# K of the last eight attention units turned on VectorE, and the phase-2 weight conversions begun one chunk earlier

## The chip, the cores and the metric

The kernel runs on one core of a Trainium2 chip. Five engines with queues of their own work side by side: TensorE (PE; its weight loads are shown apart as PEld), VectorE (DVE), ScalarE (ACT), GpSimd (POOL) and SyncE (SP), which here does nothing but issue DMAs. Within a queue instructions run in order. The metric is device time: 1471.89 us, the median of three runs (1470.66 to 1473.28).

## The reference

Three blocks follow each other, all in float32: a two-step attention through 32 packed vectors per head, a mixer with a token shift, and a mixer over tokens and channels. The first block is the one that changes:

```
def sm_attn(qq, kk, vv):
    s = scale * matmul(qq, kk.T)          # then softmax over the last axis
    return softmax(s) @ vv
p_packed = sm_attn(p, k, v)               # p: 8 x 8 x 32 x 64; k, v: 8 x 8 x 576 x 64
out = sm_attn(q, p_packed, p_packed)      # q: 8 x 8 x 576 x 64
x = out.transpose(0, 2, 1, 3)             # heads side by side: 8 x 576 x 512
k2 = relu(xk @ w_k); v2 = k2*k2 @ w_v; r = sigmoid(xr @ w_r); y = r * v2
u = y + token mixing of y with U, V;  result = u + relu(u @ w_ch1) @ w_ch2
```

`xk` and `xr` are mixes of `x` with `x` one token earlier.

## The kernel before

**Attention** is cut into 16 units, numbered by (pair of batches `bp`, pair of heads `j`): a unit has two batches times two heads. For one unit K (576 x 64 per head) has to stand with its 64 dims on the partitions before it is multiplied with the packed queries P; this turned K is the tile `kh`. Every unit loads K with four DMAs (`load_k`, L612): two of 256 KB in runs of 1 KB, two of 32 KB for the last 64 tokens. TensorE turns it: eight 128x128 transposes into two PSUM banks (L682 to L688), which ScalarE or VectorE copy to `kh`, and two 64-column transposes for the tail, copied to a part of the tile `at` (called `kt`, L690 to L696). One more transpose turns P (`pbd` to `pT`). Then come the scores (`psat<-kh,pT`, `psat<-at,pT`), their maxima, the exponentials (`a1`), and so on to `xo`, which is stored to `x_d`.

For Q the two halves of the units differ. Units 0 to 7 ("plain", `u < NPLAIN`) turn Q on TensorE too. Units 8 to 15 load Q with eight DMAs of 72 KB in runs of 128 bytes, 32 dims of one head per 32 partitions (L633 to L641), so that VectorE's transpose of 32x32 blocks (`plan.turn`, two instructions a unit) gives the layout wanted.

**The mixer** runs over 12 chunks of 384 columns (three chunks per pair of batches). A chunk has the matmul groups `psr` (36 matmuls of 512 columns), `psk` (96 of 384) and `psv` (72 of 512), and `psu`. The first four units run ahead of the mixer. Units 4 to 7 are mixed in among the matmuls of chunk 0 on, units 8 to 11 from chunk 3 on, units 12 to 15 from chunk 6 on in the program, but on the queues they stand earlier, since the last eight have the highest class (`cls = 0`, L1408).

**Casts.** The weights of phase 2 (`V`, `w_ch1`, `w_ch2`, 34 pieces) come as float64 and are converted on the side: a DMA brings a piece to a tile `st` (three buffers), ScalarE takes its absolute value, VectorE makes float32 of the bits in some six integer and float instructions with tiles `a` and `m` (two buffers each), and a DMA stores `m` to `v_d` or `w_d` (`Cast.run`, L894). From chunk `CAST0` = 2 on each chunk has `NPER` = 5 of these in its lowest class (`cls = 3`).

**Phase 2** (from about 690 us) is a chain of matmuls `psc`, with `w_d` turned into seven sums per block (`ws_d`) during chunks 7 to 10.

**What sets the order.** All instructions are recorded first and then ordered by a list scheduler (`Plan.emit`, L346) that simulates the five queues: each engine takes the ready instruction of the lowest class; TensorE and SyncE take the earliest recorded within a class. Copies out of PSUM may go to ScalarE or VectorE, whichever is free. The order that results is fixed in the program. A tile's buffers come free when its last reader is done: a unit's K tile is loaded again for the next unit once its transposes have read it. DMAs of SyncE share eight semaphores in turn, so that a DMA is issued when the eighth before it has landed.

Of the kernel before, what the change touches and what calls it, by code (L numbers as in the profile page):

```python
# [9 lines left out]
F32 = mybir.dt.float32  # L10
# [3 lines left out]
AF = mybir.ActivationFunctionType  # L14
# [470 lines left out]
def packed_attention_moe_mixer_kernel(  # L485
# [18 lines left out]
    B, H, S, D = q.shape  # L504
    NP = p.shape[2]
    P = 128
# [15 lines left out]
    NPLAIN = 2 * NJ  # L522
    SCALE = 1.0 / float(D) ** 0.5
# [3 lines left out]
    plan = Plan(nc)  # L527
# [37 lines left out]
    def ps_att():  # L565
        return plan.bank(att_banks[0], "psat", att_banks[0] is ps_a)
# [17 lines left out]
    class Bufs:  # L584
# [22 lines left out]
            return self.kept[1:]  # L607

        def tile_in(self, tag):
            return plan.tile(self.big_p, [P, 1152], F32, "big", parts=tuple(range(8)), name=tag)  # L610

        def load_k(self, u, after=()):  # L612
            bp, j = divmod(u, NJ)
            if u not in self.kin:
                self.kin[u] = self.tile_in("kin")
            t = self.kin[u]
            for b2 in range(2):
                src = k[2 * bp + b2, 2 * j:2 * j + 2]
                plan.dma(
                    t.at(b2)[:, b2 * 512:(b2 + 1) * 512].rearrange("p (h t d) -> p h t d", t=4, h=2),  # L620
                    src[:, 0:512, :].rearrange("h (p t) d -> p h t d", t=4), after=after)
            for b2 in range(2):
                src = k[2 * bp + b2, 2 * j:2 * j + 2]
                plan.dma(
                    t.at(2 + b2)[b2:P:2, 1024:1152].rearrange("p (h d) -> p h d", h=2),
                    src[:, 512:576, :].rearrange("h s d -> s h d"), after=after)
# [37 lines left out]
    def attention_steps(A, u, u_next):  # L664
        bp, j = divmod(u, NJ)
        kin, qin, vin = A.kin.pop(u), A.qin.pop(u), A.vin.pop(u)
# [3 lines left out]
        plain = u < NPLAIN  # L670
        kh = A.big(F32, "kh")
        qt, at = A.big(F32, "qt"), A.big(F32, "at", (0, 1))
        pT, ppz = A.keep(plain)
# [5 lines left out]
        if early:  # L679
            claim()  # L680

        for b2 in range(2):  # L682
            yield
            ps = ps_att()
            for n in range(4):
                plan.transpose(ps[:, n * P:(n + 1) * P],
                               kin.at(b2)[:, b2 * 512 + n * P:b2 * 512 + (n + 1) * P], ident)
            plan.copy(kh[:, b2 * 512:(b2 + 1) * 512], ps)  # L688
        yield
        ps = ps_att()  # L690
        for h in range(2):
            plan.transpose(ps[0:64, h * P:(h + 1) * P], kin[:, 1024 + h * 64:1088 + h * 64], ident)
        plan.transpose(ps[:, 2 * P:3 * P], A.pbd.rearrange("p h d -> p (h d)"), ident)
        kt = at.at(1)[:, 640:896].rearrange("p (h c) -> p h c", h=2)
        plan.copy(kt[0:64].rearrange("p h (b c) -> p h b c", b=2),
                  ps[0:64, 0:2 * P].rearrange("p (h c b) -> p h b c", h=2, b=2))  # L696
        plan.copy(pT, ps[:, 2 * P:3 * P].rearrange("p (b c) -> p b c", b=2))
        if early:
            A.load_k(u_next, A.after)
# [1 line left out]
        st = A.st  # L701
        yield
        sps = [ps_att() for _ in range(2)]
        for b2 in range(2):
            for h in range(2):
                o = slice(b2 * 64 + h * 32, b2 * 64 + (h + 1) * 32)
                for r in range(2):
                    rows = slice(r * 64, (r + 1) * 64)
                    plan.mm(sps[r][o, 0:256], pT[rows, b2, h * 32:(h + 1) * 32],
                            kh[rows, b2 * 512 + h * 256:b2 * 512 + (h + 1) * 256],  # L710
                            start=True, stop=True, skip_group_check=True)
        for b2 in range(2):
            for h in range(2):
                o = slice(b2 * 64 + h * 32, b2 * 64 + (h + 1) * 32)
                plan.mm(sps[0][o, 256:320], pT[0:64, b2, h * 32:(h + 1) * 32],
                        kt[0:64, h, b2 * 64:(b2 + 1) * 64], start=True, stop=True, skip_group_check=True)
        s0, s1 = st.at(0), st.at(1)
        plan.reduce(s0[:, 0:1], sps[0][:, 0:320], ALU.max)
        plan.reduce(s0[:, 1:2], sps[1][:, 0:256], ALU.max)
# [1 line left out]
        a1 = A.a1  # L721
        bias = st.at(0)[:, 3:4]
        for r in range(2):
            plan.act(a1[:, 0:512].rearrange("p (n r c) -> p n r c", n=2, r=2)[:, :, r, :],
                     sps[r][:, 0:256].rearrange("p (n c) -> p n c", n=2), AF.Exp,
                     st.at(1)[:, 4 + r:5 + r], bias, SCALE)
        for b2 in range(2):
            r = slice(b2 * 64, (b2 + 1) * 64)
            plan.act(a1[r, 512 + b2:640:2], sps[0][r, 256:320], AF.Exp,
                     st.at(1)[r, 6:7], bias[r], SCALE)  # L730
        plan.reduce(s0[:, 8:9], s1[:, 4:8], add)
        plan.recip(s0[:, 9:10], s0[:, 8:9])

        for c in range(3 if plain else 0):
            yield
            ps = ps_att()
# [3 lines left out]
            n = 3 if c < 2 else 2  # L740
# [6 lines left out]
        if not plain:  # L747
            yield
            for b2 in range(2):
                r = slice(b2 * S, (b2 + 1) * S)  # L750
# [5 lines left out]
        ps = ps_att()  # L756
# [4 lines left out]
        ps = ps_att()  # L761
# [4 lines left out]
        ps = ps_att()  # L766
        for t in range(5):
            for g in range(4):
                o = t * P + g * 32
# [3 lines left out]
                        start=(t == 0), stop=(t == 4), skip_group_check=True)  # L773
# [3 lines left out]
        if not plain:  # L777
            for b2 in range(2):
                r = slice(b2 * 64, (b2 + 1) * 64)
# [5 lines left out]
        ps = ps_att()  # L785
# [13 lines left out]
        if plain:  # L799
# [25 lines left out]
            ps = ps_att()  # L825
# [4 lines left out]
            ps = ps_att()  # L830
            plan.transpose(ps[:, 0:P], a2f[:, 512:640], ident)
            for b2 in range(2):
                r = slice(b2 * 64, (b2 + 1) * 64)
                plan.copy(th[r, 512:576], ps[r, r])
        else:
            n = S // NP
            a2 = plan.tile(A.one, [P, 20, NP], F32, "a2", parts=(0, 1))[:, 0:n, :]
            s2 = plan.tile(A.one, [P, 4, 20], F32, "s2", parts=(0, 1))
            for g, (c0, c1) in enumerate(halves):
                yield  # L840
                ps = ps_att()
# [19 lines left out]
        for c0, c1 in halves:  # L861
            w = c1 - c0
            if plain:
                yield
                pss = [ps_att() for _ in range(2)]
                for b2 in range(2):
                    r = slice(b2 * 64, (b2 + 1) * 64)
# [13 lines left out]
    def attention(A, u, u_next):  # L881
        for _ in attention_steps(A, u, u_next):
            pass
# [83 lines left out]
    for what in FIRST.split():  # L967
        u = int(what[1])
# [14 lines left out]
    plan.cls = 0  # L983
    A0.after = go
    steps = [attention_steps(AX_[u], u, NJ if u == 0 else None) for u in range(NLEAD)]
    step = 0
    while any(s is not None for s in steps):
# [36 lines left out]
    for b2 in range(2):  # L1024
        r = slice(b2 * 64, (b2 + 1) * 64)
# [7 lines left out]
    for i0, i1 in ((0, NI),):  # L1033
        src = uv[:, i0 * NP:i1 * NP]
# [145 lines left out]
    def tmp_tile():  # L1180
        i = count["tmp"] % 6
        count["tmp"] += 1
        if i < 3:
            return plan.tile(m_p, [P, CW], F32, "m", name="tmp")[:, 0:256]
        return plan.tile(tr_p, [P, 256], F32, "tmp")
# [148 lines left out]
    def product(q, f, i, name, fresh):  # L1334

        if fresh:
            bank_abc[name] = plan.bank(ps_c1, "psc1")
        ps = bank_abc[name][:, 0:256]
        w, x = load_ws(f, i), ops[q][i]
        n = 0  # L1340
        for k in range(2):
            for wi, a in PASS:
                plan.mm(ps, half(w, wi)[:, k * P:(k + 1) * P],
                        half(x, a).rearrange("p (a k c) -> p k a c", a=4, k=2)[:, k],
                        start=(fresh and n == 0), stop=(n == 5), skip_group_check=True)
                n += 1
        return ps
# [34 lines left out]
            plan.dma(v_d[:, c * 288:(c + 1) * 288], w[0:NP, 0:288])  # L1382
        casts.append((slice(0, NP), V[:, c * 288:(c + 1) * 288], 288, put_v))
    NCAST, FIRST_WS = 9, 7
    CAST0, NPER = 2, 5
    for m in range(MC):
        def put1(w, m=m):
            plan.dma(w1_d[m], w)
# [16 lines left out]
    for n in range(len(chunks)):  # L1405
        b, c = chunks[n]
# [27 lines left out]
        if n >= CAST0:  # L1434
            plan.cls = 3
            for _ in range(len(casts) if n == NCAST else NPER):
                if casts:
                    rows, src, size, put = casts.pop(0)
# [27 lines left out]
    for q in range(NQ):  # L1466
# [12 lines left out]
        for f in range(NF):  # L1479
# [9 lines left out]
            b = product(q, f, 1, "b", True)  # L1489
            s = tmp_tile()  # L1490
            plan.tt(s, p1, b, add)
            c = product(q, f, 2, "c", True)
# [68 lines left out]
```

## Time and profile before

| | |
|---|---|
| three runs | 1470.66, 1471.89, 1473.28 us |
| profiled execution | 1469.44 us |
| span of its instructions | 1467.7 us |
| TensorE, weight loads | 1434.1 us busy (98%), 1259.5 us (86%) |
| VectorE, ScalarE, GpSimd | 988.5 us (67%), 716.2 us (49%), 268.8 us (18%) |
| DMA | 294.53 MB, 201 GB/s in the mean |

The profiled execution takes 1.7 us more than the span of its instructions. TensorE's busy time counts matmuls from their start to a modelled end, so that it says little about free time; the spacing of the weight loads, one per matmul, says more. By the stores of `xo` the units 8 to 15 follow each other from 218.4 us to 475.8 us, each about 32 us long.

### The profile page before, as it was taken

The numbers are of one execution on the slowest core, as the hardware profiler recorded it, in microseconds if no ns is written. First come the engines' busy times: TensorE is split into PE (matmuls) and PEld (weight loads), VectorE is DVE, ScalarE is ACT, GpSimd is POOL, SyncE is SP. The second block draws the span as 40 slices with busy tenths as digits, with TensorE's granted clock in tenths as the row PEclk, the third lists the DMA queues.
The fourth block names the chain that finished last, engine by engine and source line by source line (L and its number), as shares of the span: only waits on it lengthen the run. The fifth ranks groups of instructions, "written<-read, shape, count | busy, mean of one in ns | idle before, by whom it ended". The sixth has DMA issues, their size and how long they took to land.

```text
span 1467.7 us, 25586 instructions
## 1 busy us (share of the span) xinstructions
PE 1434.1 (98%) x9104; PEld 1259.5 (86%) x9104; DVE 988.5 (67%) x2147; ACT 716.2 (49%) x1519; POOL 268.8 (18%) x519
## 2 busy tenths in 40 slices
PE   6799999999999999999999999999999999999998
PEld 5678888888888988889899999899998999999997
DVE  6999577888788888885665465556546554554533
ACT  5777656776666677664443333333223332333322
POOL 0000000000000000100333333333333333333331
PEclk8889999999999999999999999999999999999999
DMA  8864355666552877841999988899998789879763
GB/s 232 254 193 123 97 137 137 188 175 179 158 158 94 291 246 248 255 153 59 308 261 249 225 231 215 212 258 225 230 230 212 204 220 247 208 215 237 202 179 79
DMA packets 235709, 294.53 MB, mean 201 GB/s; under 512 B 91200, under 2 KB 126336, under 8 KB 235584
## 3 DMA queue, kind: packets, MB, share of 16 engines
q1 hardware_dynamic: 163008, 160.76, 37.8%
q0 software_dynamic: 72576, 132.15, 35.6%
q8 instruction: 73, 1.20, 0.3%
q14 instruction: 52, 0.43, 0.1%
HBM read 231.94 MB, written 60.89 MB: 200 GB/s over the span
## 4 chain that ended last, share of the span: by engine, by line
PE 90%; DMA 3%; DVE 3%; SPq 2%; ACT 1%; issue 1%; DVEq 0%; ACTq 0%
PE psc L197 50%; PE psk L197 13%; PE psv L197 13%; PE psr L197 7%; PE psat L197 4%; PE psat L209 2%; SPq L319 2%; PE psu L197 1%; DMA kin<-in_k_dram 1%; PE psh L197 1%; DMA st<-in_moe_w_k_dram 1%; DMA ut<-uq_d 0%; DMA st<-in_moe_w_v_dram 0%; DMA uq_d<-ux 0%; DMA w_d<-m 0%
## 5 line engine op out<-in xcount | busy, mean ns | idle before, releaser
L197 PE MATMUL psc<-w,hid 128*128 128x512 f32 x1728 | 421.1, 391 | 0.4 <-DVE hid L273 0.4
L197 PEld LDWEIGHTS psc<-ob,wb 128*128 128x128 f32 x3024 | 387.4, 191 | 13.4
L197 PE MATMUL psc<-ob,wb 128*128 128x256 f32 x3024 | 392.0, 283 | 0.0
L319 POOL DMA_DIRECT2D wb<-ws_d x504 | 266.9, 530 | 647.6 <-PE psc L197 401.5
L197 PEld LDWEIGHTS psc<-w,hid 128*128 128x128 f32 x1728 | 314.6, 188 | 60.6 <-DVE hid L273 1.5
L233 ACT ACTIVATE hid<-tmp 128x256 fp32r<-128x256 f32 x216 | 131.5, 676 | 231.0 <-DVE tmp L254 231.0
L197 PE MATMUL psk<-xk,wk 128*128 128x384 f32 x1152 | 227.1, 340 | 0.4 <-ACT sq L233 0.4
L197 PE MATMUL psv<-wv,kk 128*128 128x512 f32 x864 | 226.3, 397 | 0.0
L197 PEld LDWEIGHTS psk<-xk,wk 128*128 128x128 f32 x1152 | 201.3, 188 | 11.1 <-issue 2.6
L197 PEld LDWEIGHTS psv<-wv,kk 128*128 128x128 f32 x864 | 158.6, 188 | 32.9 <-issue 3.0
L273 DVE SCALAR_TENSOR_TENSOR hid<-tmp,hid 128x256 fp32r<-128x256 f32 x216 | 127.2, 633 | 54.6 <-ACT hid L233 54.1
L273 DVE SCALAR_TENSOR_TENSOR hid<-psc,hid 128x256 fp32r<-128x256 f32 x72 | 45.3, 629 | 167.4 <-ACT hid L233 167.4
L254 DVE TENSOR_TENSOR tmp<-tmp,psc 128x256 f32<-128x256 f32 x288 | 112.9, 409 | 61.7 <-PE psc L197 61.7
L233 ACT ACTIVATE hid<-psc 128x256 fp32r<-128x256 f32 x72 | 45.8, 636 | 157.3 <-PE psc L197 157.3
L197 PE MATMUL psr<-wr,xr 128*128 128x512 f32 x432 | 114.5, 406 | 2.0 <-DVE xr L291 1.6
L197 PEld LDWEIGHTS psr<-wr,xr 128*128 128x128 f32 x432 | 81.9, 194 | 21.3 <-DVE xr L291 2.1
L288 ACT ACTIVATE tmp<-psc 128x256 f32<-128x256 f32 x144 | 57.2, 397 | 58.7 <-PE psc L197 50.7
L233 ACT ACTIVATE sq<-psk 128x384 f32<-128x384 f32 x96 | 46.8, 489 | 75.1 <-PE psk L197 74.7
L311 POOL MEMSET x<- 128x8 f32 x4 | 0.4, 112 | 429.7 <-DVE m L270 249.2
L254 DVE TENSOR_TENSOR kk<-sq,kk 128x384 fp32r<-128x384 f32 x96 | 52.6, 549 | 25.1 <-ACT kk L288 24.6
L233 ACT ACTIVATE m<-x,om_t 128x384 f32<-128x384 f32 x96 | 55.3, 607 | 4.9 <-DVE xr L254 3.8
L270 DVE SCALAR_TENSOR_TENSOR m<-x,mu_t,m 128x384 f32<-128x384 f32 x96 | 56.4, 608 | 0.3 <-ACT m L233 0.2
(157 smaller groups left out, 1500.6 us busy)
## 6 DMA issues: line engine op xcount, KB each, us to landing
wb<-ws_d POOLq DMA_DIRECT2D x504, 256.0 KB, 4.0
st<-in_moe_w_ch_dram SPq DMA_DIRECT2D x32, 512.0 KB, 5.3
ws_d<-wb SPq DMA_DIRECT2D x56, 256.0 KB, 4.0
x_d<-xo SPq DMA_DIRECT2D x16, 576.0 KB, 3.8
x_d<-x SPq DMA_DIRECT2D x36, 256.0 KB, 2.6
kin<-in_k_dram SPq DMA_DIRECT2D x32, 256.0 KB, 4.5
vin<-in_v_dram SPq DMA_DIRECT2D x32, 256.0 KB, 4.8
x<-x_d SPq DMA_DIRECT2D x8, 1024.0 KB, 5.8
```

Source lines behind the costliest of these rows:

```text
L197: self.nc.tensor.matmul(o, l, r, start=start, stop=stop, **k)
L209: self.nc.tensor.transpose(out.get(), in_.get(), ident.get())
L233: self.nc.scalar.activation(o, in_.get(), func, **k)
L254: return self.elem(engs, lambda e, o, x, y: e.tensor_tensor(out=o, in0=x, in1=y, op=op), out, [a, b], self.TT, cls)
L270: ("dve",), lambda e, o, x, y, z: e.scalar_tensor_tensor(out=o, in0=x, scalar=z, in1=y, op0=op0, op1=op1), out, [a, b, s], {"dve": (1.042, ...
L273: ("dve",), lambda e, o, x, y: e.scalar_tensor_tensor(out=o, in0=x, scalar=s, in1=y, op0=op0, op1=op1), out, [a, b], self.TT, cls)
L288: self.nc.scalar.activation(o, i, AF.Copy)
L311: (self.nc.gpsimd if eng == "pool" else self.nc.vector).memset(o, 0.0)
L319: (self.nc.sync if eng == "sp" else self.nc.gpsimd).dma_start(out=o, in_=i)
```

## The change

Units 8 to 15 load K as they load Q: in runs of 128 bytes, 32 dims of a head on 32 partitions. That takes 24 DMAs a unit, 16 of 32 KB and 8 of 8 KB, in place of four. One transpose of VectorE over the whole tile (128 x 1152) gives `kh`, tail included; the ten transposes on TensorE, two of the three PSUM banks of the stage and the three copies of K go. The columns of `kh` come out in another order than before, so the scores read other rows for the second batch, and the exponentials write their results with a stride that restores the order. P is still turned on TensorE. Apart from this, `CAST0` is 1: the casts begin in chunk 1, five a chunk as before.

```
         def tile_in(self, tag):
-            return plan.tile(self.big_p, [P, 1152], F32, "big", parts=tuple(range(8)), name=tag)
+            return plan.tile(self.big_p, [P, 1152], F32, "big", parts=tuple(range(24)), name=tag)
...
+            if u >= NPLAIN:
+                for b2 in range(2):
+                    for h in range(2):
+                        src = k[2 * bp + b2, 2 * j + h]
+                        main = src[0:512].rearrange("(p n r) (e s) -> r e p n s", p=32, r=2, e=2)
+                        c0 = (2 * b2 + h) * 256
+                        for g in range(4):
+                            plan.dma(t.at(8 * b2 + 4 * h + g)[g * 32:(g + 1) * 32, c0:c0 + 256]
+                                     .rearrange("p (n s) -> p n s", s=32), main[g // 2 ^ b2, g % 2], after=after)
+                        tail = src[512:S].rearrange("(p n) (e s) -> e p n s", n=2, e=2)
+                        c0 = 1024 + h * 64
+                        for e in range(2):
+                            g = 2 * b2 + e
+                            plan.dma(t.at(16 + 4 * b2 + 2 * h + e)[g * 32:(g + 1) * 32, c0:c0 + 64]
+                                     .rearrange("p (n s) -> p n s", s=32), tail[e], after=after)
+                return
...
-        for b2 in range(2):
+        for b2 in range(2 if plain else 0):
             yield
             ps = ps_att()
...
         yield
+        if not plain:
+            plan.turn(kh, kin)
         ps = ps_att()
-        for h in range(2):
+        for h in range(2 if plain else 0):
             plan.transpose(ps[0:64, h * P:(h + 1) * P], kin[:, 1024 + h * 64:1088 + h * 64], ident)
         plan.transpose(ps[:, 2 * P:3 * P], A.pbd.rearrange("p h d -> p (h d)"), ident)
...
+                    rows = slice(b2 * 64, (b2 + 1) * 64)
+                    tail = kh[rows, 1024 + h * 64:1088 + h * 64]
...
+                to = to.rearrange("p n (c m) -> p m n c", m=4)
+                s = s.rearrange("p (m n c) -> p m n c", m=4, n=2)
+            plan.act(to, s, AF.Exp, st.at(1)[:, 4 + r:5 + r], bias, SCALE)
...
-    CAST0, NPER = 2, 5
+    CAST0, NPER = 1, 5
```

How the order moves is shown at three places, all around unit 9, first the one before, then the one of the changed kernel.

TensorE's queue before, from the K transposes of unit 9 (`ident,kin`) to its scores (`kh,pT` and, for the tail, `at,pT`); `psv` and `psr` are the mixer's:

```order
L209 MATMUL psat<-ident,kin 128x128 x8
L197 MATMUL psv<-wv_1113,kk 128x512 x4
L197 MATMUL psr<-wr_200,xr 128x512
L209 MATMUL psat<-ident,kin 64x128 x2
L209 MATMUL psat<-ident,pbd 128x128
L197 MATMUL psr<-wr_200,xr 128x512 x2
L197 MATMUL psr<-wr_201,xr 128x512 x3
L197 MATMUL psr<-wr_202,xr 128x512
L197 MATMUL psat<-kh,pT 32x256 x8
L197 MATMUL psat<-at,pT 32x64 x4
```

The same place now, from the last matmuls of unit 8 (`th,wide`) to unit 9's scores:

```order
L197 MATMUL psat<-th,wide 128x256 x3
L197 MATMUL psr<-wr_202,xr 128x512 x2
L209 MATMUL psat<-ident,pbd 128x128
L197 MATMUL psv<-wv_1114,kk 128x512 x4
L197 MATMUL psr<-wr_202,xr 128x512
L197 MATMUL psat<-kh,pT 32x256 x8
L197 MATMUL psat<-kh,pT 32x64 x4
```

The ten transposes of K are gone and only that of `pbd` is left between the units; the tail's scores now read `kh`.

VectorE's queue before, where unit 9's second half of K is copied (`kh<-psat`, then the tail `at<-psat`), up to the maxima of its scores (`st<-psat`); `st<-a` and `a<-a` belong to a cast, `m` and `xr` to the mixer:

```order
L264 TENSOR_SCALAR st<-a 128x512
L264 TENSOR_SCALAR a<-a 128x512
L291 COPY kh<-psat 128x512
L270 SCALAR_TENSOR_TENSOR m<-x,mu_t,m 128x384 x2
L291 COPY at<-psat 64x256
L270 SCALAR_TENSOR_TENSOR m<-x,mu_t,m 128x384
L254 TENSOR_TENSOR xr<-m,xr 128x384
L277 TENSOR_REDUCE st<-psat 128x1
L254 TENSOR_TENSOR xr<-m,xr 128x384
L277 TENSOR_REDUCE st<-psat 128x1
```

VectorE's queue now, where unit 9's K is turned; `pp`, `wide`, `a_2845` and `s_2826` are unit 8's:

```order
L270 SCALAR_TENSOR_TENSOR pp<-psat,st,hmask 128x128
L254 TENSOR_TENSOR kk<-sq,kk 128x384
L254 TENSOR_TENSOR wide<-pp,wide 64x128 x2
L215 STREAM_TRANSPOSE kh<-kin 128x1152
L215 STREAM_TRANSPOSE a_2845<-psat 128x320
L215 STREAM_TRANSPOSE a_2845<-psat 128x256
L270 SCALAR_TENSOR_TENSOR m<-x,mu_t,m 128x384
L277 TENSOR_REDUCE s_2826<-a_2845 128x18
```

The one transpose of K has moved about half a unit ahead: it stands in the middle of unit 8, in front of unit 8's own turned scores.

SyncE's queue before, from the store of unit 7's `xo` on: K and Q of unit 9 (`kin`, `qin`), then x of a chunk, a cast's load (`st`) and store (`v_d`):

```order
L319 DMA x_d_66<-xo 128x1152
L319 DMA kin<-in_k_dram 128x2x256 x2
L319 DMA kin<-in_k_dram 64x2x64 x2
L319 DMA qin<-in_q_dram 32x18x32 x8
L319 DMA x<-x_d_66 128x384
L319 DMA x<-x_d_66 128x2x63
L319 DMA st<-in_moe_w_ch_dram 128x4x256
L319 DMA v_d<-m 32x288
L319 DMA st<-in_moe_w_ch_dram 128x4x256
L319 DMA vin<-in_v_dram 128x2x256
```

SyncE's queue now, at K and Q of unit 9:

```order
L319 DMA kin<-in_k_dram 32x8x32 x4
L319 DMA kin<-in_k_dram 32x2x32 x2
L319 DMA kin<-in_k_dram 32x8x32 x4
L319 DMA kin<-in_k_dram 32x2x32 x2
L319 DMA kin<-in_k_dram 32x8x32 x4
L319 DMA kin<-in_k_dram 32x2x32 x2
L319 DMA kin<-in_k_dram 32x8x32 x4
L319 DMA kin<-in_k_dram 32x2x32 x2
L319 DMA qin<-in_q_dram 32x18x32 x8
L319 DMA x_d_66<-xo 128x1152
L319 DMA st<-in_moe_w_ch_dram 128x4x256 x2
L319 DMA w_d_81<-m 128x512
```

K's four DMAs have become 24, and what follows them, the store of `xo`, two cast loads and a cast's store (`w_d_81`), stands behind 32 DMAs of K and Q where it stood behind 12.

## Rows read from the trace of the kernel before

**Rows 1.** the page's chain that ended last: shares of the span by engine.

```profile
PE 90%; DMA 3%; DVE 3%; SPq 2%; ACT 1%; issue 1%; DVEq 0%; ACTq 0%
```

**Rows 2.** busy time by stage: window, length, engines (instructions), clock, DMA share, GB/s.

```profile
135.10:195.30 60.20, 59.74 (x393) 48.90 (x392) 38.59 (x90) 36.27 (x83) 0.00 (x0) 1.00 0.38 105
218.40:475.80 257.40, 254.40 (x1788) 214.73 (x1787) 215.64 (x477) 172.19 (x383) 0.32 (x2) 1.00 0.54 156
250.80:283.90 33.10, 32.20 (x223) 26.43 (x222) 28.77 (x63) 24.74 (x53) 0.00 (x0) 1.00 0.66 192
564.40:607.30 42.90, 42.90 (x212) 38.20 (x211) 38.49 (x88) 29.81 (x64) 5.42 (x10) 1.00 0.91 284
```

**Rows 3.** weight loads by form, 218 to 476 us: busy, mean ns, idle before.

```profile
L197 PEld LDWEIGHTS psk<-xk,wk 128*128 128x128 f32 x448 | 77.9, 188 | 4.8 <-issue 1.1 <-ACT sq L233 0.7
...
L209 PEld LDWEIGHTS psat<-ident,kin 128*128 128x128 f32 x64 | 7.4, 140 | 1.2 <-ACT xo L288 0.4
L209 PEld LDWEIGHTS psat<-ident,kin 128*64 128x64 f32 x16 | 1.8, 110 | 0.9
...
L209 PEld LDWEIGHTS psat<-ident,pbd 128*128 128x128 f32 x8 | 1.1, 140 | 0.0
```

**Rows 4.** weight loads of one unit's K stage in order: start, us, what.

```profile
250.88 1.03 PEld L209 LDWEIGHTS psat<-ident,kin 128*128 128x128 f32 x8
251.88 0.77 PEld L197 LDWEIGHTS psv<-wv,kk 128*128 128x128 f32 x4
...
252.93 0.34 PEld L209 LDWEIGHTS psat<-ident,kin 128*64 128x64 f32 x2
253.27 0.14 PEld L209 LDWEIGHTS psat<-ident,pbd 128*128 128x128 f32 x1
...
254.97 0.18 PEld L197 LDWEIGHTS psat<-kh,pT 64*32 64x32 f32 x16 [0.36 <-issue]
```

**Rows 5.** the K tile's copies out of PSUM, 218 to 460 us: ns min/median/max.

```profile
L288 ACT ACTIVATE kh<-psat x9: 580/596/598, 252.2 to 445.0; 128x512 f32<-128x512 f32 x9
L291 DVE COPY kh<-psat x7: 672/691/692, 219.1 to 412.3; 128x512 f32<-128x512 f32 x7
```

**Rows 6.** VectorE's transposes and K's tail copy, whole run.

```profile
L215 DVE STREAM_TRANSPOSE ux<-u 128x512 f32<-128x512 f32 x32 | 22.3, 696 | 0.1
L215 DVE STREAM_TRANSPOSE qt<-qin 128x576 f32<-128x576 f32 x16 | 12.3, 771 | 0.0
...
L291 DVE COPY at<-psat 64x256 f32<-64x256 f32 x7 | 2.9, 414 | 0.9 <-PE psat L209 0.6
```

**Rows 7.** SyncE's queue through one unit: start, us, what.

```profile
250.78 0.33 SPq L319 DMA_DIRECT2D x_d<-xo  x1
251.21 2.71 SPq L319 DMA_DIRECT2D kin<-in_k_dram  x4
253.96 5.95 SPq L319 DMA_DIRECT2D qin<-in_q_dram  x8
...
283.03 0.34 SPq L319 DMA_DIRECT2D xu_d<-xu  x1
```

**Rows 8.** issue times on SyncE's queue: Q as loaded for units 8 on.

```profile
L319 SPq DMA_DIRECT2D qin<-in_q_dram x64: 577/630/1542, 187.6 to 420.2; - x64
```

**Rows 9.** the same of the mixer's x loads.

```profile
L319 SPq DMA_DIRECT2D x<-x_d x13: 319/432/622, 227.3 to 432.4; - x13
```

**Rows 10.** one stall on a store, in order; idle before in brackets.

```profile
397.80 0.64 SPq L319 DMA_DIRECT2D w_d<-m  x1
...
401.49 0.43 DVE L264 TENSOR_SCALAR m<-a 128x512 int32<-128x512 int32 x1 [3.91 <-DMA w_d<-m]
...
407.50 0.30 PEld L197 LDWEIGHTS psat<-th,wide 128*128 128x128 f32 x2 [1.50 <-ACT th L233]
```

**Rows 11.** who waited for whom, 218 to 476 us: total, times, longest.

```profile
DVE m L264 <- DMA w_d<-m: 5.2, 2, 3.9
...
DVE m L264 <- DMA v_d<-m: 2.1, 2, 1.4
```

More of the change, by code (lines that the diff above doesn't have):

```diff
@@ L694, in attention_steps @@
         kt = at.at(1)[:, 640:896].rearrange("p (h c) -> p h c", h=2)
-        plan.copy(kt[0:64].rearrange("p h (b c) -> p h b c", b=2),
-                  ps[0:64, 0:2 * P].rearrange("p (h c b) -> p h b c", h=2, b=2))
+        if plain:
+            plan.copy(kt[0:64].rearrange("p h (b c) -> p h b c", b=2),
+                      ps[0:64, 0:2 * P].rearrange("p (h c b) -> p h b c", h=2, b=2))
         plan.copy(pT, ps[:, 2 * P:3 * P].rearrange("p (b c) -> p b c", b=2))
@@ L707, in attention_steps @@
                 for r in range(2):
-                    rows = slice(r * 64, (r + 1) * 64)
+                    rows = r if plain else r ^ b2
+                    rows = slice(rows * 64, (rows + 1) * 64)
                     plan.mm(sps[r][o, 0:256], pT[rows, b2, h * 32:(h + 1) * 32],
@@ L714, in attention_steps @@
                 o = slice(b2 * 64 + h * 32, b2 * 64 + (h + 1) * 32)
-                plan.mm(sps[0][o, 256:320], pT[0:64, b2, h * 32:(h + 1) * 32],
-                        kt[0:64, h, b2 * 64:(b2 + 1) * 64], start=True, stop=True, skip_group_check=True)
+                if plain:
+                    rows, tail = slice(0, 64), kt[0:64, h, b2 * 64:(b2 + 1) * 64]
+                else:
+                    rows = slice(b2 * 64, (b2 + 1) * 64)
+                    tail = kh[rows, 1024 + h * 64:1088 + h * 64]
+                plan.mm(sps[0][o, 256:320], pT[rows, b2, h * 32:(h + 1) * 32], tail,
+                        start=True, stop=True, skip_group_check=True)
         s0, s1 = st.at(0), st.at(1)
@@ L723, in attention_steps @@
         for r in range(2):
-            plan.act(a1[:, 0:512].rearrange("p (n r c) -> p n r c", n=2, r=2)[:, :, r, :],
-                     sps[r][:, 0:256].rearrange("p (n c) -> p n c", n=2), AF.Exp,
-                     st.at(1)[:, 4 + r:5 + r], bias, SCALE)
+            to, s = a1[:, 0:512].rearrange("p (n r c) -> p n r c", n=2, r=2)[:, :, r, :], sps[r][:, 0:256]
+            if plain:
+                s = s.rearrange("p (n c) -> p n c", n=2)
+            else:
+                to = to.rearrange("p n (c m) -> p m n c", m=4)
+                s = s.rearrange("p (m n c) -> p m n c", m=4, n=2)
+            plan.act(to, s, AF.Exp, st.at(1)[:, 4 + r:5 + r], bias, SCALE)
         for b2 in range(2):
             r = slice(b2 * 64, (b2 + 1) * 64)
-            plan.act(a1[r, 512 + b2:640:2], sps[0][r, 256:320], AF.Exp,
-                     st.at(1)[r, 6:7], bias[r], SCALE)
+            to, s = a1[r, 512 + b2:640:2], sps[0][r, 256:320]
+            if not plain:
+                to, s = to.rearrange("p (c m) -> p m c", m=2), s.rearrange("p (m c) -> p m c", m=2)
+            plan.act(to, s, AF.Exp, st.at(1)[r, 6:7], bias[r], SCALE)
         plan.reduce(s0[:, 8:9], s1[:, 4:8], add)
```

## The prediction

> **What bounds the kernel now.** I read the chain that ended last first: 90% of it is TensorE [rows 1], so I looked for places where TensorE does not follow itself closely. The busy time by stage gives the levels [rows 2]. In a chunk without attention (564 to 607 us) TensorE is busy for all of 42.9 us, its weight loads for 38.2. In the stretch of units 8 to 15 (218.4 to 475.8 us, 257.4 us long) the weight loads fill only 214.7 us, VectorE is busy for 215.6 us (84%) and ScalarE for 172.2 us (67%). The granted clock is 1.00 in both, the upper of the two levels, 2.4 GHz, and no row here gives a reason for it to change. So this stretch is the one where a second engine could matter. The weight loads by form [rows 3] show how much: their 14 groups, from `psk` to `pbd`, have 43.2 us of idle time before them, and the releasers that the rows name (ScalarE 0.7 and 0.4 us in those shown) are a small part of it. TensorE is the limit, with a looser schedule in this stretch than after it. Everything behind the stretch hangs on TensorE alone, so what is saved here should come out at the end.
>
> **The change part by part.** The sums are for the profiled execution, 1469.44 us with a span of 1467.7 us; it lies 2.45 us under the median of the runs shown, 1471.89 us, and I carry differences over to that median.
>
> *TensorE loses K's transposes.* In unit 9 the eight large ones hold it from 250.88 to 251.88 us, 1.00 us, and the two of the tail from 252.93 to 253.27 us, 0.34 us [rows 4]. That is 1.34 us a unit and 10.7 us for eight units. From the other side, the weight loads of these 80 instructions are busy for 7.4 + 1.8 = 9.2 us [rows 3]. I take 10.7 us, since the spacing is what the next matmul waits for. The transpose of P stays and costs what it did.
>
> *VectorE gets one transpose of 1152 columns a unit.* No row shows this length. From 512 to 576 columns the time goes from 696 to 771 ns [rows 6], 1.17 ns a column, which gives 771 + 576 x 1.17 = 1.45 us; twice the row of 576 gives 1.54 us. I take 1.45 us, as one start is saved: 11.6 us for eight. Seven of the sixteen `kh` copies go from VectorE, 7 x 0.69 = 4.8 us, and nine from ScalarE, 9 x 0.60 = 5.4 us [rows 5]; of the tail's copies VectorE had seven in the whole run at 0.414 us [rows 6] and in the new order has two, which saves 2.1 us. That would leave VectorE with 4.7 us more. But copies may go to either engine, and over the whole new order VectorE also does five copies of `xo` and five casts of `kk` fewer, so that it ends near nothing. I take 0; the bounds are 0 and 4.7 us, if all of it reached TensorE. The turn stands in the middle of the unit before, in front of that unit's own scores, so unit 8's path gets 1.45 us longer there. TensorE has mixer matmuls to do meanwhile; with no such cover it would be 8 x 1.45 = 11.6 us.
>
> *A unit's own path gets shorter.* Its K stage, from the first transpose at 250.88 us to the scores at 254.97 us, is 4.1 of the unit's 33.1 us [rows 2, 4]. Where this shows, it shows as less idle time on TensorE. I take 0 and make it a rival.
>
> *SyncE gets 20 more DMAs a unit.* In the unit shown it issues for 18.4 us of 33.1 (the sum of twelve rows, from 0.33 us for the store of `xo` to 0.34 us for `xu`), 2.71 us of it for K's four and 5.95 us for Q's eight [rows 7]. A DMA of 32 KB in 128-byte runs is not in the trace. Q's are the nearest in form, 0.63 us each [rows 8]; the mixer's loads of x, with one or two runs per partition, take 0.432 us in the median and 0.319 us at least [rows 9]. By the shortest the 24 need 7.7 us, by Q's 15.1 us. I take Q's for the 16 main pieces and the x loads' for the 8 tail pieces with two runs: 16 x 0.63 + 8 x 0.432 = 13.5 us. SyncE then issues for 18.4 - 2.7 + 13.5 = 29.2 us a unit. With 1.34 us less on TensorE a unit is some 31.8 us long, so the queue holds, at 92%, but has little room left. K, Q and V are wanted a whole unit after they are asked for: turning K needs data that was asked for some 30 us earlier, and 13.5 us of issue and the landing fit in that. What does suffer is short work queued behind K and Q, above all the casts' loads and stores: up to 10.8 us later. A cast's next instruction on VectorE needs the tile `m` that the store two casts earlier is reading, and a wait there blocks all of VectorE's queue.
>
> The price of one such wait is in the trace. Up to 401.49 us VectorE stood still for 3.91 us for a store that was issued at 397.80 us; TensorE went on with mixer matmuls and lost 1.50 us once, at 407.50 us, when the turned scores came late [rows 10]. In the stretch there are four such waits, 7.3 us together [rows 11]. The scheduler puts a landing time on every DMA and places casts behind it, so I don't expect one per unit. I take one more than before: 1.5 us. The ends are 0 and two per unit, 16 x 1.5 = 24 us.
>
> *Casts from chunk 1 on.* In chunk 1 VectorE is busy for 38.6 of 60.2 us [rows 2], and two of the five casts that go there are the small ones of V. Even at six instructions of 0.69 us, the longest of `kh`'s copies taken for each, five casts are 20.7 us and fit into the 21.6 us that are free. At the other end of the line four casts leave the chunks where TensorE has no idle time to win. Cost 0. The bounds: if the two waits for stores of V [rows 11] vanish, 3.0 us are won at 1.5 us each; if each of the five casts causes one, 7.5 us are lost.
>
> *The small edits.* The tail's scores are as many matmuls as before. The exponentials write the same elements with a stride; no row shows ScalarE writing so. Taken at 0, and at 3 us to both sides with the next stage's matmuls as the cover.
>
> The sum: 10.7 us saved, 1.5 us given back, 9.2 us. The span becomes 1458.5 us, the profiled execution 1460.2 us, the median 1462.7, so 1463 us.
>
> **The rivals.** *A, the queue of SyncE.* K's small transfers fill SyncE; each unit's casts find their buffers late, VectorE stops, and TensorE loses 1.5 us each time. For it: in the new order each unit has two to three cast transfers behind K and Q, and Q's own 0.63 us for all 24 would fill 30.8 us of 31.8. Against it: TensorE bore the wait of 3.91 us with a loss of 1.50 us, and the four waits so far come to 7.3 us in eight units. It ends slower from the eighth wait on (8 x 1.5 = 12.0 us against 10.7 saved); two a unit give 1471.9 - 10.7 + 24 = 1485 us, one a unit 1473 us. The Trainium skill, "DMA: Bandwidth & Descriptors", section "Rules for kernel authors", speaks for this rival: transfers under 64 KB should be merged, since they are nearly all overhead, which would make a piece of 8 KB as dear as one of 72 KB. The trace agrees so far as it goes: Q's 72 KB pieces and K's mean of 0.68 us for pieces of 32 and 256 KB lie close together [rows 7], and by that 0.68 us the 24 would need 16.3 us and SyncE 32 us a unit, just over its length.
>
> *B, the unit's path.* If TensorE's idle time in the stretch, 43.2 us, goes with the length of the units, 4.1 of 33.1 us off each take 43.2 x 0.124 = 5.4 us more: 1462.7 - 5.4 = 1457 us. For it: idle time is there in this stretch and hardly at all in the chunk without attention. Against it: 1.45 us of the turn go into the path again, and VectorE is at 84%.
>
> *C, VectorE as the bound.* TensorE's saved time becomes waits for VectorE: 4.7 us more of it if the copies don't even out, and the turn's 1.45 us in each unit's path. 4.7 us, with the 1.5 us for SyncE and half of the path's 11.6 us, give 12.0 us against 10.7: 1473 us, no change to speak of. For it: the 84%. Against it: the releasers named in rows 3.
>
> **How the numbers follow.** What this kernel can tell from no change is about 0.2%, 2.9 us. My forecast, 1463 us with a range of its own of 1458 to 1468, has a chance of 0.53, B 0.17, C 0.13, A 0.17. The first two are faster by more than 2.9 us: 0.70. C is within it: 0.13. A is slower: 0.17. The range goes from 1454 us (B, and the 3 us of the small edits or of V's casts) to 1477 us, which takes in C and the first third of A.
>
> **What would show it.** Right: 80 transposes `ident,kin` fewer, eight VectorE transposes of 128 x 1152 near 1.45 us, the end of the last unit about 10 us earlier and the later stages shifted by as much at the same length. Wrong: K's DMAs on SyncE near 0.7 us each, waits of VectorE for `w_d` stores above 15 us in total or of ScalarE for cast loads, a stretch of units as long as before; or chunks after the last unit longer than 42.9 us.

## The result, and the profile after the change

The changed kernel takes 1480.03 us (median of four runs, 1478.97 to 1481.81) against 1471.28 us for the kernel before beside it: a ratio of 1.0065, 95% interval 1.0039 to 1.0091. It is 0.65% slower, where 1463 us was forecast. The profiled execution took 1480.22 us with a span of 1478.5 us.

The chain that ended last has TensorE at 87%, three points lower than in [rows 1], and SyncE's queue at 3%:

```profile
PE 87%; DVE 4%; DMA 3%; SPq 3%; ACT 1%; issue 1%; DVEq 0%; ACTq 0%
```

To find the stage that grew, cut the span where each mixer chunk's first `psr` matmul starts. The rows are the changed kernel's chunks 2 to 7 and the time from phase 2's first matmuls on (window, length, engines, granted clock, DMA share, GB/s):

```profile
194.00:261.10 67.10, 61.03 (x378) 48.58 (x377) 40.76 (x88) 36.13 (x81) 0.11 (x1) 0.90 0.57 141
261.10:314.80 53.70, 53.70 (x392) 45.12 (x391) 47.81 (x100) 38.32 (x88) 0.00 (x0) 1.00 0.55 142
314.80:374.80 60.00, 56.08 (x385) 45.68 (x385) 46.59 (x104) 35.97 (x81) 0.00 (x0) 0.97 0.57 149
374.80:432.50 57.70, 55.15 (x354) 45.93 (x352) 45.53 (x95) 36.37 (x82) 0.11 (x1) 0.97 0.58 150
432.50:484.90 52.40, 52.40 (x365) 44.33 (x363) 47.63 (x102) 36.17 (x77) 0.20 (x1) 1.00 0.50 154
484.90:527.80 42.90, 42.90 (x211) 38.20 (x210) 37.75 (x87) 31.95 (x69) 0.00 (x0) 1.00 0.86 292
...
702.10:1478.50 776.40, 770.13 (x4804) 695.58 (x4803) 424.10 (x882) 257.41 (x500) 260.98 (x493) 1.00 0.86 221
```

The same cut of the kernel before, for the chunks that grew, chunk 7 and the last stage:

```profile
195.30:252.90 57.60, 56.86 (x393) 47.53 (x392) 43.66 (x100) 34.80 (x74) 0.11 (x1) 1.00 0.44 125
...
308.10:364.40 56.30, 56.30 (x414) 47.50 (x414) 49.53 (x109) 39.64 (x91) 0.00 (x0) 1.00 0.64 186
364.40:419.60 55.20, 53.84 (x359) 45.91 (x358) 46.70 (x102) 36.03 (x80) 0.11 (x1) 1.00 0.54 149
...
472.40:516.60 44.20, 44.20 (x221) 39.49 (x220) 38.35 (x87) 31.46 (x68) 0.00 (x0) 1.00 0.77 266
...
690.90:1467.70 776.80, 770.13 (x4804) 695.62 (x4802) 423.51 (x882) 256.96 (x499) 260.98 (x493) 1.00 0.87 220
```

Chunk 2 is 9.5 us longer (67.1 against 57.6), chunk 4 3.7 us and chunk 5 2.5 us. Chunk 7 starts 12.5 us later than before (484.9 against 472.4 us) and is 1.3 us shorter; the stages behind it keep their lengths, so that 10.8 us arrive at the end of the span. The three chunks that grew are also the three whose granted clock is below 1.00.

In chunk 2 the reason can be followed from queue to engine. First SyncE's queue (start, us, what):

```profile
187.96 16.93 SPq L319 DMA_DIRECT2D kin<-in_k_dram  x24
...
206.09 5.33 SPq L319 DMA_DIRECT2D qin<-in_q_dram  x8
...
212.64 2.98 SPq L319 DMA_DIRECT2D x<-x_d  x6
215.73 2.45 SPq L319 DMA_DIRECT2D vin<-in_v_dram  x4
218.22 1.69 SPq L319 DMA_DIRECT2D st<-in_moe_w_ch_dram  x3
220.01 19.14 SPq L319 DMA_DIRECT2D kin<-in_k_dram  x24
239.25 5.29 SPq L319 DMA_DIRECT2D qin<-in_q_dram  x8
244.65 0.56 SPq L319 DMA_DIRECT2D x_d<-xo  x1
```

K's 24 DMAs hold the queue for 16.9 and 19.1 us, where [rows 7] have 2.71 us for four; with Q's eight behind them little else gets out. Three loads of weights to be converted (`st`) leave at 218.2 us, all together. The store of `xo`, whose last copy on ScalarE ended at 234.2 us, leaves at 244.65 us. ScalarE meets the late loads in its fixed order (idle time before an instruction in brackets, with its releaser):

```profile
223.23 0.67 ACT L233 ACTIVATE a<-st 128x512 f32<-128x512 f32 x1 [4.12 <-DMA st<-in_moe_w_ch_dram]
225.76 0.66 ACT L233 ACTIVATE a<-st 128x512 f32<-128x512 f32 x1 [1.86 <-DMA st<-in_moe_w_ch_dram]
226.32 0.92 ACT L288 ACTIVATE th<-psat 128x512 f32<-128x512 f32 x3
```

The copy of `th`, which attention needs, stands behind two conversions in ScalarE's queue. TensorE waits for it:

```profile
227.05 0.74 PEld L197 LDWEIGHTS psat<-th,pp 64*128 64x128 f32 x4 [4.64 <-ACT th L288]
```

Then the clock, in steps around that wait (columns as in the windows above):

```profile
218.40:225.00 6.60, 4.45 (x25) 3.74 (x23) 2.68 (x6) 1.34 (x3) 0.00 (x0) 1.00 0.96 288
225.00:230.00 5.00, 2.95 (x7) 1.89 (x8) 3.17 (x8) 3.00 (x7) 0.00 (x0) 0.56 0.40 70
230.00:235.00 5.00, 5.00 (x11) 2.31 (x11) 1.75 (x4) 0.77 (x2) 0.00 (x0) 0.50 0.20 31
235.00:240.00 5.00, 5.00 (x38) 3.78 (x38) 2.10 (x6) 0.47 (x2) 0.00 (x0) 0.57 0.25 37
240.00:245.00 5.00, 5.00 (x29) 4.57 (x28) 2.32 (x7) 4.28 (x13) 0.00 (x0) 1.00 0.60 93
```

The granted clock falls during the idle 4.64 us. Window means of 0.56, 0.50 and 0.57 are what 4.4, 5.0 and 4.3 us at 0.50 give, the lower level of 1.2 GHz: 13.7 us, until about 239 us. The ten microseconds from 230 to 240 us hold what 5.4 us would hold at 1.00 (5 x 0.50 + 5 x 0.57), which is 4.6 us lost.

For the whole of chunk 2 an estimate from the windows comes near its 9.5 us. TensorE is idle (length less busy time) for 6.1 us against 0.7 us before, and a clock of 0.90 costs at most 6.7 us of 67.1. From these 12.1 us the transposes of two units go off that stood in this chunk before, 2.7 us by the prediction's price.

Over all eight units the waits for DMAs read as follows (186 to 485 us; total, times, longest):

```profile
ACT a L233 <- DMA st<-in_moe_w_ch_dram: 16.6, 5, 5.2
...
DVE m L264 <- DMA w_d<-m: 6.1, 3, 3.5
...
DVE kh L215 <- DMA kin<-in_k_dram: 1.5, 1, 1.5
...
DVE qt L215 <- DMA qin<-in_q_dram: 1.3, 1, 1.3
```

In the kernel before, ScalarE's wait for those loads was 5.4 us in five times. VectorE's for stores, 7.3 us in [rows 11], has not grown.

### The profile page after: what moved, and what is told of

It reads as the page before. It is cut to its first block, busy times and chain, and to the rows that moved or that the text cites. A ratio compares the mean times of both kernels' runs of the same rounds, so it can differ in the third digit from the quotient of the medians.

```text
span 1478.5 us, 25599 instructions
## 1 busy us (share of the span) xinstructions
PE 1436.4 (97%) x9024; PEld 1256.3 (85%) x9024; DVE 988.3 (67%) x2125; ACT 718.9 (49%) x1525; POOL 268.9 (18%) x519
## 4 chain that ended last, share of the span: by engine, by line
PE 87%; DVE 4%; DMA 3%; SPq 3%; ACT 1%; issue 1%; DVEq 0%; ACTq 0%
PE psc L197 51%; PE psk L197 12%; PE psv L197 11%; PE psr L197 6%; PE psat L197 4%; SPq L319 3%; PE psat L209 1%; DMA st<-in_moe_w_ch_dram 1%; PE psu L197 1%; DMA kin<-in_k_dram 1%; PE psh L197 1%; DMA st<-in_moe_w_k_dram 1%; ACT a L233 0%; DVE m L270 0%; DVE s L277 0%
## 5 line engine op out<-in xcount | busy, mean ns | idle before, releaser
L197 PEld LDWEIGHTS psc<-ob,wb 128*128 128x128 f32 x3024 | 387.4, 191 | 13.4
```

The lines of the kernel that those rows point to most:

```text
L197: self.nc.tensor.matmul(o, l, r, start=start, stop=stop, **k)
```

## The experiments

Thirteen kernels were timed beside the kernel before (1470.3 to 1471.6 us in the four groups); each median is of 4 to 12 executions. The last column is (ratio - 1) x 1471 us, so that runs of different groups can be set against each other; most intervals are 1 to 2 us to either side, those of e1, e7 and e8 2.5 to 3, that of the changed kernel 3.8. Every edit also makes the planner write another order, so a difference of 2 or 3 us is not by itself the effect of what was edited: e12, which alters the order alone, moves the kernel before by 1.6 us.

| run | K turned by | K's DMAs a unit, queue | conversions from chunk | us | ratio, 95% interval | us to before |
|---|---|---|---|---|---|---|
| changed kernel | VectorE | 24, SyncE | 1 | 1480.03 | 1.0065 [1.0039, 1.0091] | +9.6 |
| e1_k_only | VectorE | 24, SyncE | 2 | 1510.21 | 1.0274 [1.0257, 1.0291] | +40.3 |
| e2_casts_only | TensorE | 4, SyncE | 1 | 1474.47 | 1.0019 [1.0006, 1.0032] | +2.8 |
| e3_k_pool | VectorE | 24, GpSimd | 1 | 1465.52 | 0.9966 [0.9953, 0.9979] | -5.0 |
| e4_k_8dma | VectorE | 8, SyncE | 1 | 1467.89 | 0.9980 [0.9968, 0.9991] | -2.9 |
| e5_k_8dma_c2 | VectorE | 8, SyncE | 2 | 1468.73 | 0.9987 [0.9977, 0.9996] | -1.9 |
| e6_k_pool_c2 | VectorE | 24, GpSimd | 2 | 1467.11 | 0.9982 [0.9972, 0.9992] | -2.6 |
| e7_split24 | TensorE | 24, SyncE | 1 | 1490.78 | 1.0146 [1.0128, 1.0163] | +21.5 |
| e8_casts_pool | VectorE | 24, SyncE | 1, loads on GpSimd | 1477.64 | 1.0055 [1.0034, 1.0075] | +8.1 |
| e9_gap650 | VectorE | 24, SyncE | 1, spacing 0.65 | 1472.74 | 1.0016 [1.0006, 1.0027] | +2.4 |
| e10_k8_pool | VectorE | 8, GpSimd | 1 | 1466.97 | 0.9971 [0.9961, 0.9981] | -4.3 |
| e11_k_4dma | VectorE | 4, SyncE | 1 | 1462.75 | 0.9946 [0.9932, 0.9959] | -7.9 |
| e12_before_gap650 | TensorE | 4, SyncE | 2, spacing 0.65 | 1468.70 | 0.9989 [0.9981, 0.9998] | -1.6 |
| e13_8dma_gap650 | VectorE | 8, SyncE | 1, spacing 0.65 | 1465.22 | 0.9966 [0.9954, 0.9978] | -5.0 |

**e1_k_only and e2_casts_only: each half of the change alone.**

```diff
 e1, from the changed kernel         e2, from the kernel before
-    CAST0, NPER = 1, 5             -    CAST0, NPER = 2, 5
+    CAST0, NPER = 2, 5             +    CAST0, NPER = 1, 5
```

> The changed kernel with the casts begun in chunk 2 again; K is turned on VectorE and loaded with 24 DMAs a unit as before this run. Queue theory (24 DMAs of about 0.7 us fill SyncE for 16 to 19 of a unit's 32 us, cast transfers land late, ScalarE and VectorE wait for them in order, TensorE idles): K's block on SyncE stays at 16 to 19 us, the time stays at 1474 to 1482 us. Casts theory (the three cast loads pulled in front of unit 9's K did it): about 1461 us, and no wait of ScalarE for cast loads above 5 us. VectorE theory (the turn itself costs it): 1478 to 1482 us.

> The kernel before with the casts begun in chunk 1 and nothing else. Queue theory and VectorE theory: within 3 us of before, 1468 to 1474 us, since SyncE has room. Casts theory: 1478 to 1482 us.

The early conversions cost the kernel before 2.8 us, so they don't explain the loss. But K's half without them is 30.7 us slower still, which none of the three theories expected. Most of those microseconds stand just ahead of phase 2: its first matmul comes at 728.0 us against 702.1 us in the changed kernel, while the last mixer chunk starts only 3.7 us later (660.5 against 656.8). Windows of e1 around it:

```profile
645.00:690.00 45.00, 45.00 (x222) 40.08 (x221) 38.48 (x77) 28.67 (x55) 0.00 (x0) 1.00 0.50 169
690.00:728.00 38.00, 23.67 (x99) 18.22 (x98) 26.31 (x50) 12.69 (x25) 0.00 (x0) 0.77 0.51 164
```

TensorE is idle for 14.3 of 38 us, and the granted clock falls to 0.77, while VectorE finishes conversions: their last store leaves at 717.2 us, in the changed kernel at 650.1 us. With the 24 DMAs on SyncE the conversions fall so far behind that, in the changed kernel, the early start saves 30.7 us.

**e3_k_pool, e4_k_8dma: SyncE relieved in two ways.**

```diff
 e3:
-  plan.dma(t.at(...)..., main[...], after=after)
+  plan.dma(t.at(...)..., main[...], after=after, eng="pool")
 ...   (and so for the tail's pieces)
 e4 (K as Q is loaded; the scores of head h read partition half h):
+  src = k[2 * bp + b2, 2 * j + h].rearrange("(t r) (e s) -> e r t s", r=32, e=2)
+  for e in range(2):
+      plan.dma(t.at(...)[g * 32:(g + 1) * 32, b2 * S:(b2 + 1) * S]..., src[e], after=after)
```

> The changed kernel with K's 24 DMAs a unit issued from GpSimd's queue, which is idle in this part, instead of SyncE's. Queue theory: SyncE issues for 16 us a unit, ScalarE's waits for cast loads go back to about 5 us, and the time is 1460 to 1465 us. VectorE theory and casts theory: 1478 to 1482 us, no better than the changed kernel.

> The changed kernel with K loaded by 8 DMAs of 72 KB a unit, exactly as Q is: each head's 64 dims on one half of the partitions, columns in the order of the tokens, so that the scores of a head read the half of that head. Casts from chunk 1 on, the turn on VectorE stays. Queue theory: K's block on SyncE takes 8 x 0.7 = 5.6 us in place of 16 to 19, time 1460 to 1465 us. VectorE theory and casts theory: 1478 to 1482 us.

Both are faster than before, with the turn still on VectorE. From 186 to 485 us ScalarE waits for conversions' loads for 0.3 us in e3 and 1.1 us in e4, against 16.6 us. e3 is the plainest test: with the same 24 DMAs of the same bytes and runs on another queue 14.6 us are won (+9.6 to -5.0, the two intervals together some 4 us), so it is not the bytes or the short runs that cost the time. Each DMA takes about as long on GpSimd's queue (the row, of seven units: ns min/median/max), but GpSimd had only 0.32 us of work in this stretch [rows 2]:

```profile
L319 POOL DMA_DIRECT2D kin<-in_k_dram x168: 533/582/1494, 208.6 to 397.4; - x168
```

**e5_k_8dma_c2, e6_k_pool_c2: the later start with SyncE relieved.** The edit is `CAST0` from 1 to 2, in e4 and in e3.

> The changed kernel with K loaded by 8 DMAs per unit, as Q is, and the phase-2 weights converted from the third chunk on, as before the change. If the loss came from SyncE's queue alone, this is the K half of the change with the queue relieved: the early conversions cost the kernel before 2.9 us by themselves (1474.5 against 1471.6), so 1467.9 - 2.9 = 1465 us, between 1462 and 1468. The rival: shorter units leave less room for the conversions, so that a later start makes phase 2 wait for them, as in the run with 24 DMAs and the later start (1510 us): then 1475 us or more.

> The changed kernel with K's 24 DMAs per unit on GpSimd's queue and the conversions from the third chunk on. Queue theory: 1465.5 - 2.9 = 1462.6 us, between 1460 and 1466. Rival as in the run with 8 DMAs: a later start of the conversions makes phase 2 wait, 1473 us or more.

Both miss their numbers: the 2.9 us don't come off. With a relieved queue the later start comes out 1.0 and 2.4 us the wrong way, about as much as the intervals allow for no effect, and the 31 us of e1 do not recur. What the start of the conversions is worth thus hangs on the queue.

**e7_split24: the DMAs alone.** TensorE still turns K; only its four loads are cut.

```diff
+  for g in range(8):
+      rows = slice(g * 16, (g + 1) * 16)
+      plan.dma(t.at(8 * b2 + g)[rows, ...]..., main[rows], after=after)
 ...
+  for e in range(4):
+      plan.dma(t.at(16 + 4 * b2 + e)[e * 32 + b2:(e + 1) * 32:2, 1024:1152]..., tail[...], after=after)
```

> The kernel before, conversions from the second chunk on, K of the last eight units still turned by TensorE, but its four loads per unit cut into 24 of the same bytes (16 partitions each). Queue theory: the 24 DMAs alone make the loss; changed kernel 1480 against 1466.7 for the two runs with SyncE relieved is 13 us, on top of 1474.5 for the kernel before with early conversions: 1484 to 1492 us, with ScalarE waiting for the conversions' loads. Rival (VectorE's turn, or the scores' and exp's new layout, makes the loss): 1473 to 1477 us.

It came out at 1490.8 us, 18.7 us over e2: the DMAs alone lose more than the whole change does. The same wait shows, larger than in the changed kernel:

```profile
ACT a L233 <- DMA st<-in_moe_w_ch_dram: 21.5, 6, 8.2
...
DVE m L264 <- DMA w_d<-m: 7.3, 5, 2.2
```

**e8_casts_pool: the conversions' loads out of SyncE's order.**

```diff
-  plan.dma(to, src, after=after)
+  plan.dma(to, src, after=after, eng="pool" if put is not None else "sp")
```

> The changed kernel with all its 24 K DMAs left on SyncE, but the loads of the weights to be converted (34 in all) issued on GpSimd's queue. If what hurts is that these loads stand behind the K block in SyncE's order and ScalarE and VectorE then wait for them: 1465 to 1471 us. If what hurts is that the block delays the units' own loads (K, Q, V, x) or the stores: 1476 to 1482 us.

1477.6 us: moving these loads wins 1.5 us, inside the intervals. The loss moved: in e8's stretch from 200 to 218 us it is VectorE's turn of K that finds its data missing, and TensorE waits behind it (the transpose of P hangs on `pp`, which VectorE makes after the turn):

```profile
DVE kh L215 <- DMA qin<-in_q_dram: 6.3, 1, 6.3
PE psat L209 <- DVE pp L270: 6.1, 1, 6.1
```

The first row names Q's DMAs, but the first of these, issued at 206.65 us, landed at 213.3 us, after the turn had begun at 211.7. What the turn waited for was K: its last two pieces, issued at 203.9 and 204.6 us, landed 6.8 and 7.0 us later, where 2.3 us is the changed kernel's median. Three loads of 512 KB, issued from GpSimd between 202.3 and 204.6 us, were on the way with them, and the DMA engines' share was 0.92 from 206 to 212 us. So e8 put a new stall in place of the old one, and shows that moving the loads does not cure the change; it does not show how much of the loss had gone by their place behind the block.

**e11_k_4dma: the turn with no more DMAs than before.**

```diff
-            if u >= NPLAIN:
-                for b2 in range(2):
-                    for h in range(2):
-  ...
-                return
```

> The changed kernel with K loaded by the four DMAs of before, so that SyncE carries nothing more; K's rows then stand in another order than the scores take them in, which is left so. It shows what the turn on VectorE is worth with no queue cost: by the prediction's 10.7 us, against 1474.5 for the kernel before with early conversions, 1463 to 1465 us. If only part of TensorE's saving is on the path, as the run with 8 DMAs (1467.9) says if 4 more DMAs cost nothing: 1466 to 1469 us.

1462.75 us. e11 leaves out the new order of K's rows, so it measures time only. The turn on VectorE is worth 10.7 us (e11 at -7.9 against e2 at +2.8; the intervals together some 3 us), and the 20 DMAs cost 17.5 us (the changed kernel's +9.6 against -7.9; some 4 us). Of these, e3 gets 14.6 back by the other queue; the 2.9 us from e3 to e11 are about what their two intervals allow for nothing.

The windows show in what form the time is lost. e11's chunks 2 to 6, cut as above:

```profile
193.60:248.50 54.90, 54.86 (x377) 45.36 (x376) 42.98 (x92) 36.80 (x81) 0.11 (x1) 1.00 0.62 167
248.50:302.50 54.00, 54.00 (x394) 45.45 (x393) 46.20 (x102) 38.22 (x86) 0.00 (x0) 1.00 0.62 177
302.50:356.90 54.40, 53.71 (x386) 44.97 (x385) 47.38 (x102) 37.45 (x83) 0.00 (x0) 1.00 0.64 179
356.90:411.00 54.10, 53.05 (x348) 44.29 (x347) 48.24 (x103) 34.46 (x76) 0.11 (x1) 1.00 0.54 141
411.00:466.60 55.60, 54.48 (x368) 44.67 (x367) 49.02 (x107) 38.44 (x85) 0.20 (x1) 1.00 0.48 163
```

TensorE is idle for 2.9 us in these and for 12.5 us in the changed kernel's chunks 2 to 6. The clock is 1.00 here and cost there at most 10.2 us (0.10 x 67.1 + 0.03 x 60.0 + 0.03 x 57.7). The two differences, 9.6 and 10.2 us, come to 19.8 us, against 18.3 us between the two spans: by this estimate, waits and the lower clock that goes with them have about equal parts in the loss.

**e9_gap650, e12_before_gap650, e13_8dma_gap650: the order planned for the true spacing.** The planner spaces DMAs by 0.50 us in the attention part; one number is changed, and with it only the order.

```diff
-    LEAD = (60.0, 500.0, 1.0, 1700.0)
+    LEAD = (60.0, 650.0, 1.0, 1700.0)
```

> The changed kernel with one number of the planner altered: it spaces SyncE's DMAs of the attention part by 0.65 us instead of 0.50, near what the K DMAs take (0.68 to 0.80). Only the order of instructions changes. If SyncE's time itself makes the loss, the order can win back little: 1474 to 1482 us. If the loss comes from an order made for landings that are too early (ScalarE and VectorE reach conversions and turns whose data are not there): 1464 to 1471 us.

> The kernel before, with the planner's spacing of SyncE's DMAs at 0.65 us instead of 0.50, as a control of the run that did so to the changed kernel (1472.7 against 1480.0). If that gain came from an order that now fits the 24 DMAs, it is not to be had here: 1468 to 1474 us. If 0.65 is simply the better number for any order: 1461 to 1466 us.

> The changed kernel with K loaded by 8 DMAs per unit on SyncE and the planner's spacing at 0.65 us. If the 5 us between 8 DMAs (1467.9) and 4 (1462.8) come from an order planned for shorter blocks of loads: 1462 to 1466 us, the fastest correct kernel of the study. If they are SyncE's time: 1466 to 1470 us.

The number wins 7.2 us in the changed kernel, 1.6 us in the kernel before and 2.1 us with 8 DMAs. So some 5 us of the 17.5 came from an order that expected the 24 DMAs' data too early (an estimate; the intervals together allow 4 us to either side). In e9's execution chunk 2 runs at a granted clock of 1.00, and only chunk 4 at 0.97. e9 landed between its two ranges: a truer order helps, but does not bring back the whole loss.

**e10_k8_pool: the fewest DMAs on SyncE.** The edit is `eng="pool"` on e4's eight K DMAs.

> The changed kernel with K loaded by 8 DMAs per unit, issued on GpSimd's queue. SyncE then carries 4 DMAs per unit fewer than before the change. If SyncE's time is still worth something there: 1461 to 1465 us, below both the run with 8 DMAs on SyncE (1467.9) and the one with 24 on GpSimd's queue (1465.5). If these two are already free of the queue: 1465 to 1468 us.

1466.97 us, not below e3. e3 has no K DMA on SyncE either, so this pair only shows that 8 or 24 of them on GpSimd's queue come to the same; against e4, taking the eight off SyncE wins 1.4 us, inside the intervals. Apart from e11, whose K rows stand in another order, e3 and e13 are the fastest of the study, 5.0 us (0.34%) under the kernel before, with e10 inside their intervals.

## Why the prediction was wrong, step by step

- **TensorE's saving, 10.7 us: right.** Only ten weight loads of `ident,kin` are left after 186 us, those of unit 7. e11 against e2 gives 10.7 us, and the changed kernel against e7, both with 24 DMAs, 11.9 us. The intervals together are some 3 and 5 us, so that agreement to a tenth is luck.
- **VectorE's turn, 1.45 us and a net of 0: right.** The row has 1.375 us, and with e11's saving no more and no less than the transposes rivals B (more than the transposes) and C (VectorE as the bound) both fall:

```profile
L215 DVE STREAM_TRANSPOSE kh<-kin x8: 1367/1375/1379, 206.4 to 442.9; 128x1152 f32<-128x1152 f32 x8
```

- **Casts from chunk 1, 0: 2.8 us lost in e2**, inside the bounds (3.0 us won, 7.5 us lost). But the term was priced without the other half: beside the 24 DMAs the early start saves 30.7 us (e1).
- **SyncE, 13.5 us for the 24 DMAs: mis-sized.** The tail pieces were priced by the x loads, 0.432 us. But all pieces cost about what Q's do; the row has the 192 DMAs of eight units:

```profile
L319 SPq DMA_DIRECT2D kin<-in_k_dram x192: 560/606/1575, 188.0 to 434.7; - x192
```

  A nearer row than the x loads was in the trace of the kernel before: K's own pieces of 32 KB there, in runs of 256 bytes, took 0.61 us each (those of unit 9, at 252.6 and 253.3 us). With that the sum is 15.0 us; the eight units measure 15.0 to 16.1. With the steps between them a block takes 16.1 to 19.1 us, as far as rival A's 16.3 us and beyond. The rule of the Trainium skill that the prediction set beside rival A ("DMA: Bandwidth & Descriptors", "Rules for kernel authors") says that small transfers should be merged, as under 64 KB they are mostly overhead. The trace agrees: pieces of 8 and 32 KB cost nearly as much queue as Q's of 72 KB (medians of 0.593, 0.607 and 0.630 us).
- **"The queue holds, at 92%": the wrong question.** SyncE's idle rows from 218 to 476 us add up to 150.2 us before and 60.6 us after: it is free for a quarter of the stretch even now. What harms is a block of 22 to 24 us (24 DMAs for K, 8 for Q) that nothing can pass. That K is wanted some 30 us after it is asked for held for seven turns, none of which waited more than 0.2 us; the first, unit 8's, began 1.5 us after the last K DMA's issue and had waited 1.5 us. The prediction had the delay ("up to 10.8 us later"; the store of `xo` above left 10.5 us late) and then took it for harmless.
- **"I take one more than before: 1.5 us": this step failed.** In its place stand 17.5 us (e11 to the changed kernel; 18.7 in e7). The price came from one stall of VectorE behind a store, which TensorE bridged with mixer work. The stall that came was on ScalarE, behind a load, with an attention copy behind it that TensorE needed at once: 4.64 us in chunk 2, and then 4.6 us or more by a clock that the prediction saw no reason to doubt. Waits of ScalarE for such loads were among the prediction's own signs of being wrong, but no term priced them. The ground given for "not one per unit", that the planner puts a landing time on every DMA, failed too: its times were 0.50 us apart for DMAs that take 0.61 us and more, and putting that right wins 7.2 us.
- **Rival A was the case**, with its place (SyncE) right and its mechanism half right: the loss goes not by waits for buffers on VectorE, each at 1.5 us (those waits did not grow), but by what comes late in a fixed order, the conversions' loads for ScalarE above all. That A's 1473 to 1485 us take in 1480 is therefore luck in the price.

How the remaining 10 to 12 of the 17.5 us divide among the loads that come late is open: no run took the delay off K, Q, V and x one by one. The clock's part is read from rows and was not tried by itself, but the lower clock is there in every execution of the changed kernel: the mean granted clock is 0.979 to 0.982 in its four, and 0.985 to 0.991 in all those of the kernel before that ran beside the experiments.

## What to carry to other kernels

When work moves to another engine by way of the layout, count the DMAs that the layout needs and price each by the dearest small DMA of that queue; then ask how long the block is and what stands behind it in the same order, not how full the queue is. A stall taken from the trace is a price only for stalls of the same engine with the same work behind it: look at what is queued behind the waiting instruction. Where a planner writes the order, give it the spacing that the trace shows before judging the change.

## What the runs showed of the hardware that was not expected

- A DMA issue on SyncE costs about the same for 8, 32 and 72 KB in 128-byte runs (medians of 0.593, 0.607 and 0.630 us). e7's pieces of the same sizes have longer runs: 32 KB in runs of 1 KB took 0.422 us in the median, 8 KB in runs of 256 bytes 0.592 us. Some take much longer (2.0 us at most), so that e7's mean is 0.53 us and its block of 24 still holds the queue for 13.4 to 16.4 us, against 16.1 to 19.1 us.
- During one wait of 4.64 us on TensorE the granted clock fell to 0.50 and stayed there for 13.7 us, although the engine was at work again for most of them; nine `psv` matmuls took 628 ns (median) there, against a mean of 401 ns over the run.
